# Output projection of a recurrent-memory attention in feature quarters, summed over all heads in PSUM, with a new instruction order

## The chip, the cores and the metric

The kernel runs on one core of one Trainium2 chip. The metric is device time in microseconds of one execution of the whole program, from the host's inputs in HBM to the output in HBM. A profiled execution gives, beside its own time, a span (first to last instruction) and a trace of every instruction and DMA packet. The engines are PE (TensorE, with its weight loads shown apart as PEld), DVE (VectorE), ACT (ScalarE), POOL (GpSimd) and SP (SyncE, which here only issues DMAs).

## The reference, cut to what matters

Two attentions read the same x (2048 tokens, 512 features) and a sigmoid gate mixes them. Attention A is recurrent: 64 segments of 32 tokens, one after the other, and eight memory rows that each segment hands to the next.

```python
for s in range(n_seg):                                # 64 segments of 32 tokens
    h = jnp.concatenate([mem, xs], axis=1)            # 8 memory rows + 32 tokens
    q = jnp.einsum('btd,dhe->bhte', h, Wq)            # 32 heads of 128; k and v likewise
    scores = jnp.where(mask, jnp.einsum('bhqe,bhke->bhqk', q, k) * scale, -1e9)
    o = jnp.einsum('bhqk,bhke->bhqe', _softmax(scores), v)
    o = jnp.einsum('bhte,hed->btd', o, Wo)            # the output projection
    mem = o[:, :M, :]                                 # to the next segment
    outs.append(o[:, M:, :])
# B: 32 heads of 16 in 4 blocks of 512 tokens, softmax plus a running linear memory, then @ wo
return g * a + (1 - g) * b                            # g = sigmoid((x * gate_w).sum(-1))
```

## The kernel before

**How A is tiled.** A segment's 40 rows are 8 memory rows and 32 tokens. Only 32 of them are in the recurrence for every step: 24 tokens and the 8 memory rows (tile `hT`, 512 features as 4 chunks of 128 by 32 columns). The last 8 tokens of a segment (the "rest") are projected for four segments at once (`p_rest`), outside the recurrence. Most matmuls use the array as four column groups of 32 (mode "c32"): the stationary operand has 32 columns, its product lands in PSUM partitions 32g to 32g+31, and four such matmuls run side by side. Mode "r32" splits the rows instead, mode "full" uses the array whole; an op with mode FLEX may take c32 (four times the instructions) or full.

**One segment (`p_seg`).** `project` computes k, q and v for two halves r of 16 heads each (`wproj`, line 1401: 16 matmuls of 512 columns per half). ACT or DVE copies each result to SBUF (`copy`, line 1001), DVE transposes 32x32 blocks (line 1466). `p_s` writes a mask product (`H`, from `hide` and `neg`) and adds the scores (`S`, lines 1481 and 1485); ACT takes exp into `PT`, 160 columns for the segment's own keys and 64 for the rest rows' keys. `p_u` sums over keys with a matmul against `ones` (`U`, line 1504), ACT forms the reciprocal as exp(-ln), DVE and POOL normalize `PT` (lines 1512, 1515). `PV` and `PW` (lines 1546, 1555) give the heads' outputs, copied to `OT`.

**The output projection (`wo`, line 1300).** Eight pieces, one for four heads each. For each head two matmuls of 256 columns go to column groups 2q and 2q+1, where q is the head's parity: even heads add up in PSUM partitions 0 to 63 (two feature halves of 32 rows), odd heads in 64 to 127. The two partial sums are then brought together in two ways. For the memory rows: a copy of the whole 128x256 result to SBUF (`par`), an f32 matmul against the small selection matrix `fold` that adds the halves and transposes (`fold`, line 1024 by way of `mm`, 16 weight loads and 16 matmuls in the trace), and a copy into the next `hT` (`hm`, line 1323). For the tokens: a DVE addition of both parts (`row`, line 1330) and a DMA to the DRAM tensor `a_rows`. The rest rows take the same `wo` with no fold.

**What orders the work.** The whole program is unrolled. Every op is declared once with what it reads and writes; the order of the ops on each engine is a compressed list, `ORDER`, that is decoded by `sequences`. Work of attention B (`bq`, `bk`, `bV`, `bL`, `bPV`, ...), of the rest rows (`rk`, `rq`, `rv`, `wor`) and of the output rows (`brow`) stands between the ops of the recurrence, so that PE has something to do while ACT and DVE work on the chain. A planner in `schedule` walks the given order with assumed costs, picks PSUM banks, and settles for a FLEX op whether it runs as c32 or full; among its constants are `LATENCY`, `TO_PE`, and, for PE's code, `BLOCK = 256`, `FETCH` and `FLOOD`: it assumes that PE passes a block of 256 instructions no faster than one in `FETCH` us (`FLOOD` while the weights are loaded).

```python
            at = (int((issued - self.BLOCK_AT) // self.BLOCK) + 1) * self.BLOCK + self.BLOCK_AT
            while at <= issued + n:
                tb = t + late + dur * (at - issued) / n
                if tb < last + wait:
                    late += last + wait - tb
```

Of the kernel before, what the change touches and what calls it, by code (L numbers as in the profile page):

```python
# [8 lines left out]
ALU = mybir.AluOpType  # L9
# [10 lines left out]
    "FP%vG5*AFh`)@=8NnCc#T7)p8{2I#Njbli?Ht<MlCV0E_2Lgd>Reicq#{zej<2(WYtcaYcfL=mzo<b^n`oQrt?4X=l0K|A;jYSjkffA_2MFVM6SfEMX^o@in&({YaCYOW$y`)p7D"  # L20
    "S`XiW8t_aqvKqjW{{7CHnNq!}ps?b<?`R*wI}B4o9BGDCQx}lccl|wAQsx#w{o02*@C?H*nhOpKFwQr|H)O2w?}{*(xL7i>^Ow;17;L=E6Uiuf7ORCqgCn5CVV*y)c>XNdyXQC&8"
    "+Y72_;!n^%v+zWkK>Q@Ko%!kq_yRP(Z#qJVwdIw8L)k~B$+4;xv_U_r96XPubB_I5D2!~a2}dp1JvLq@gWDhOdm=<**9v?sxJW25Ym?-ldeoxX!x`4-3l+>aiqjY*kKt=fdyyMrS"
    "TtKi`-Q|l8k2%X9cZ`c^&x5D1fH0$}`K-Y19{9|K0owjuuA~MQY~T9tV}(4D~NG=u6&MiY&(Y)ds*WfKih3Y5+XW8~DJ8n4rAi61zX|fPX3h>*sPY#?253SEIsV1Hk8!_{Fs%!nQ"
    "XbL@>yhz*P#id{eO=GyuC3I7pc!iC#F>x^|MNu9I~d942j2BKs}C{32?UUb0LFQ0ix-*wE`Wywhw40;SaxR(xH&0w&1~3r>%^+Q~*1w%X0dLK`~oRiUZ%v@YZ{<={$P$O>#Ht-g5"
    "W_?5ZV8Q)X6FKfa2uH#n*1->#gx`OOrGTS3=MBIgi05c@<lVI(bMKO(!P|IwkpyRX!0q9ky<A$_0F>qr~Z`i)*Pf7ko@^0+Ebu=O`6HS4D0zHsqF%|pCbq*x&7jftOc|B(>)Ul5$"
    "KZkl{cAySxd)nCa4`?xYI8Ydc-J`?j)*Ub>l_L53X(X=*iUSH*O)~7hZzt}07vPzsz=lT9d}LFYhY-VCz%g-Sk&Tdn#%}I-!r0;ryuSkmW=ndEhe6SCNkfQele4rTz@yN|bXC7X5"
    "{J?2%yvEGvj;w-nk4KLC-en4_WIY7iDIe*l{w;mHRx|tg>Hls*GGYd1hEQaKs1Q}WW<p1#~=%4@4Jyoy%+bJlSOafyRp_Xa4`#}?irSp1pk9MQq0GYpf9%!-z_SyD|7gBZ%B5TIq"
    "j09gbnawgKX$c#?|1Cs~gEHo!)LH84CffGH0VZT0$^?t^N$w830B|hK2#$tvh^^sW`y7ue)i_0Lx#2>;^cu>5W;-xd<!l97zIn;Kf(ek&7pZQ+7YB*SmTARuV{y-AwMMCKM1LYPP"
    "~))4IWaaGge4THwmP{^wvY!*lvJH(bT~67Xw$Rb#i-yJ6bZqrpAMCqpVq+CL^KX1>vZdW9hs0a&MX{9>MDOZ)R2yhq84)`!GpUJj{u>>cvyS0!<>j?=fe0?v}Q=Z<x@?wNUY$yZA"
    "zFPco@wd?LO2?m!oCp7uI?No{xf`T7mh(Vuka2P2NBjL6@&q4tn9-LUHbLvQ<mFTs0mU8w)fQ=)Tg95Y{pjmMvz9MhukU!<q>{^889C|HXya@J>msYn;Tl_Dv*39cH1&mo+Xe41Y"  # L30
    "-wSm-uVZSP0nU3c{&z|2*8u<9e)|_x{U6>^pl7v3#2Y5&Q0%_`roFvjdeSO!h*#aoFJaTRlWAg97R_;xOeeX3z-(9QdN}SDbR{UFCKc&eeOa*yIPK9s9P}2;t504CtmqX2Mw+iQ5"
    "@tKA=UflNik^qvi@F+4>L0)d(&!xk19$q(bRtIQWc@BSEx8e4y#yo$@6;zSCHbBOeZ<h6B!k<!-TSDxi4K*bikZ>pp~bl>Hqu#;4C5khfUzc#d<{t6?Px5m@jG!{EB_;XNdZ7Qa<"
    "_!tG*Vk&axoj=Q&KKgrGm_PfnATjB4lFLmlBPB8c|}{Fyc`a!-M(--zSkAhMb15|1nJS3ZI?~)7F2ydR(h4w*wifi(X$wk(c`}2lq(`n}~xm+tBe-phxR7hhP(F6%c_@3;2VOi8K"
    "0IWF}OGVoT9$D^z(mhuGUFN0eV{=&U*2KX%suN4|}cpN2o&L-b5#@Rdbk@U_Uld7ja8CV1^97EpLuk<t{Q59&T~*dNd`ZCe)KF;h&EwpriKdS!qG(~F?89a_L8NS*sgg4{@w?9l;"
    "feF-5D;?)*{K|f(}k-=ex`hV8A4~wYvlG_?UwX_CM;_f^|$mxlPvs==7yyp`s7Rb6~lv|=m<wQ*l<ksWBnG4WVTD%Uxy$`QF_L4ruWV>?|lmt;to=NS1Nc$BYcj!UB54s5&=+Z`h"
    "$6zq69SP2@b??e*C23Q(rlubAYG8Kh^MNI?GS<9D)_fw_W7&0PK8f;Cos*$W35lw;%+>UwMr<%PCrT1YJNla0KLRbALfVDbK>(VU0j1RCm9-9{rB@y*uHjiUFW9VgGA^-k;>dHxG"
    "eR$#lS^p{D*pQ~>17(+Y+@-b^rsDx*={Cnd=_*+90SJ#TY=UyiMCKojX!UJ6&GV|2aE<D0SLbUunkTR!|2Xm&PGX)kcZKF97ZT}|3r-1$3e-Nix|aRz^HYTOA*=4?*hl#4A`Q<ZC"
    ">FDSD|guH5?1h>+t@Kh*e)whO4?`H0f^525@Hd0T-*mLjqyP>Zv+DfZUo#u)sNO2r~5eQv&P&Ly2AwE(f_|I)F!!J~v>^Byd`RgNXacR6P4&@1ICR>mFv;8_2B&;xuq-jliAi1`y"
    "QiKxl(&bdbgm@+%jcTuWwH?C?}<KK;o+M`hp)fJ{ZBF7r)qa0}*7TT!AH2hLiAaNOmJ{L5hEUldHLZB8`Nn5fbf=aurgjSY9}=Cci-km(4F6>u<xnAt7S&d&da+`QD8Hd9m`@PAf"
    "i&U7Qf=7yxr3w`Wwpo`F{o4zP+#qf+-LpkzF1W7Mbg_W?J-#G-CU1lgEyDqw@ap8OrJFWol3c>aYFKUY7srBDZVKt_rXp-LnMRD2U5SJsTB_R9`RO)kp49l%cJ!fZ$&-=jhuD|L%"  # L40
    "y1IUvdzTEm-vL`Z29Oo8L4yauZ2~m^KkLz9E=C6p9~IB`Pd(L|p~L8+Bvv(^n2M(!qD_IvnXdOQgQ+LnC;oNI;()5(e;6J^Ix3=lKHKpkud&+*-qK+<?LAHz3IfD{nP3vL)m#`P%"
    "Az-nXxd79gj-ZTOY~ZssKMsNKbP{8mm>eCN5+d@bU9APlO@&%!)?+M1dv$KWu03m5O+^)TKirSE&UrOh#t1H282!iaJ?N_SyYf%rosL26SCQ=!v(yq47)#|vx&cv(H<$HgxXp=hZ"
    "2Rc&T>3VCqo>V5)bn`2h({Xl$<t=(LR4S4MVUe3V}q8op9@Lb$IR$pOxMuvL-je(~;MgBrrtSk<bU9BgVhTrgb}j!lAf@3|ZWb=ET&9xiA?8xV5(vQKl#k-ESru$T<VEo5RY5VB9"
    ";n)ICN-=;*U8u9Pxj8tCC-BpAUsZ37POobHh=y4yT`df2_XjG0)I&swks>^5Y!-}`l^h^wO7;Ovx5R<w~st3jh8jw7J5Y4EKg65tqoiZL5JL9r23)xZ{hUw@x3sEOV1pE~UFC`K~"
    "E6o~y85AcZW4>C!5R`4k0&Hh@U@drH+qp{ic1@XZ_Jev2;69t(qyI`J^5hYWAkuf?5K+7OejE>t4rV5PYOVAtN`!|>%h9}RpX5a|yrwrdb;8eW!--=b((!2GHnVQzU{=A<23o^Yq"
    "ca1cMH6dYhqqEO?+;p-pDh$~Ik?)QD4#mxwHD}i19fK}G^;8&n<-!kt*dcW=w`)kd<Q*$pWyEA{*?bvSf6i3q3T)N>8khzUn-Y=>b%GL;-a8w~x(uX6%4qkp4jh=4Ls<Ne^U*ga!"
    "{Gsyolt7waUkaOTHX1Wj80I!RG%`O#TeTRWz6O1O2x#+)X$7g(DRq0Y>ZZC1q){;eHD*WCUX`%YIE&>kHDlG;q2uoJb#J}aw0jc_Cm*<UxGR3UCxAYZZ+GIsZ4seqaiJjU+FFwa$"
# [90 lines left out]
class Slot(Res):  # L138
# [446 lines left out]
class Kernel:  # L585
# [837 lines left out]
    def p_seg(self, s):  # L1423
# [13 lines left out]
        def bank():  # L1437
            return P.slot("A")
# [178 lines left out]
```

## Time and profile before

| what | value |
|---|---|
| runs shown | 829.01, 830.72, 834.39 us; median 830.72 |
| profiled execution | 832.89 us, span 831.2 us, mean granted TensorE clock 0.998 |
| PE busy | 809.5 us (97%), 24474 matmuls |
| weight loads (PEld) busy | 521.5 us (63%), 24474 |
| DVE, ACT, POOL busy | 617.3, 562.9, 260.9 us (74, 68, 31%) |
| DMA queue q8 (PE's code) | 192 packets, 3.15 MB |
| first 60 us or so | the 16 MB of A's weights are loaded, 341 to 414 GB/s |

Busy time of PE is modelled: matmuls are pipelined, each is shown with its whole latency, and a stretch that reads as fully busy may still hold short stops. The weight loads (PEld) show those stops better, since each is short. "issue" as a releaser means that the engine waited for nothing that the profile shows.

### The profile page before, as it was taken

The numbers are of one execution on the slowest core, as the hardware profiler recorded it, in microseconds if no ns is written. First come the engines' busy times: TensorE is split into PE (matmuls) and PEld (weight loads), VectorE is DVE, ScalarE is ACT, GpSimd is POOL, SyncE is SP. The second block draws the span as 40 slices with busy tenths as digits, with TensorE's granted clock in tenths as the row PEclk, the third lists the DMA queues.
The fourth block names the chain that finished last, engine by engine and source line by source line (L and its number), as shares of the span: only waits on it lengthen the run. The fifth ranks groups of instructions, "written<-read, shape, count | busy, mean of one in ns | idle before, by whom it ended". The sixth has DMA issues, their size and how long they took to land.

```text
span 831.2 us, 53272 instructions
## 1 busy us (share of the span) xinstructions
PE 809.5 (97%) x24474; PEld 521.5 (63%) x24474; DVE 617.3 (74%) x1398; ACT 562.9 (68%) x1278; POOL 260.9 (31%) x576
## 2 busy tenths in 40 slices
PE   9999999999999999999999999999999999999987
PEld 4445666666666566666666666666766665666654
DVE  4688667768778768678676687776878767886776
ACT  3577676777766667776667766676656677767663
POOL 3443231323322332323233233423232223323340
PEclk9999999999999999999999999999999999999999
DMA  9983111121111111111011111100111100000001
GB/s 341 414 247 52 40 24 43 43 45 27 43 28 28 39 28 44 27 34 44 15 47 46 38 27 31 40 14 18 44 42 32 39 20 15 13 23 23 22 21 36
DMA packets 71701, 45.63 MB, mean 55 GB/s; under 512 B 50046, under 2 KB 69942, under 8 KB 69942
## 3 DMA queue, kind: packets, MB, share of 16 engines
q1 hardware_dynamic: 70422, 41.18, 17.5%
q8 instruction: 192, 3.15, 1.6%
q10 hardware_dynamic: 1056, 1.05, 0.4%
q14 instruction: 31, 0.25, 0.1%
HBM read 30.72 MB, written 8.87 MB: 48 GB/s over the span
## 4 chain that ended last, share of the span: by engine, by line
PE 87%; DVE 4%; ACT 3%; DMA 2%; issue 1%; SPq 1%; POOL 0%; DVEq 0%; POOLq 0%
PE pb L1401 47%; PE pb L1300 17%; PE pb L1024 7%; PE pb L1141 4%; PE pb L1026 2%; PE pb L1546 2%; PE pb L1182 2%; DMA st<-in_A_mem_dram 2%; PE pb L1504 2%; PE pb L1481 1%; PE pb L1230 1%; PE pb L1555 1%; DVE KT_sb L1466 1%; PE pb L1485 1%; ACT rc_sb L1510 1%
## 5 line engine op out<-in xcount | busy, mean ns | idle before, releaser
L1001 ACT ACTIVATE st<-pb 128x512 bf16<-128x512 f32 (+2 forms) x313 | 149.0, 494 | 103.0 <-PE pb L1401 78.0
L1159 ACT ACTIVATE PTB<-pb 128x640 bf16<-128x640 f32 x240 | 158.4, 703 | 37.2 <-PE pb L1141 32.5
L1401 PE MATMUL pb<-Wv_sb,hT 128*32 128x512 bf16 x2048 | 162.8, 381 | 0.2 <-DVE ao L1330 0.2
L1401 PE MATMUL pb<-Wq_sb,hT 128*32 128x256 bf16 (+1 forms) x3072 | 138.0, 308 | 0.1
L1300 PE MATMUL pb<-Wo_sb,OT_sb 128*32 128x256 bf16 x4096 | 132.8, 273 | 3.0 <-issue 1.9
L1401 PE MATMUL pb<-Wk_sb,hT 128*32 128x512 bf16 x2048 | 132.0, 379 | 0.1
L1300 PEld LDWEIGHTS pb<-Wo_sb,OT_sb 128*32 128x32 bf16 x4096 | 100.7, 96 | 18.4 <-ACT OT_sb L1001 4.3
L1165 POOL TENSOR_SCALAR_AFFINE_SELECT PTB<-PTB 128x512 bf16<-128x512 bf16 x120 | 77.6, 647 | 107.4 <-ACT PTB L1159 100.8
L1515 POOL TENSOR_TENSOR PT_sb<-PT_sb,rc_sb 128x64 bf16<-128x64 bf16 x90 | 33.1, 367 | 248.9 <-ACT rc_sb L1510 240.5
L1401 PEld LDWEIGHTS pb<-Wq_sb,hT 128*32 128x32 bf16 x3072 | 82.5, 97 | 39.1 <-issue 0.8
L1466 DVE STREAM_TRANSPOSE QT_sb<-st 128x256 bf16<-128x256 bf16 (+1 forms) x192 | 94.4, 510 | 16.7 <-ACT st L1001 15.1
L1466 DVE STREAM_TRANSPOSE KT_sb<-st 128x512 bf16<-128x512 bf16 x128 | 89.4, 700 | 11.6 <-ACT st L1001 9.5
L1001 ACT ACTIVATE OT_sb<-pb 128x320 bf16<-128x320 f32 (+1 forms) x140 | 58.1, 428 | 37.9 <-PE pb L1555 36.3
L1401 PEld LDWEIGHTS pb<-Wk_sb,hT 128*32 128x32 bf16 x2048 | 57.0, 97 | 42.4 <-ACT PTB L1159 1.1
L1001 DVE CAST OT_sb<-pb 128x320 bf16<-128x320 f32 (+1 forms) x120 | 56.8, 478 | 31.3 <-PE pb L1555 29.3
L1401 PEld LDWEIGHTS pb<-Wv_sb,hT 128*32 128x32 bf16 x2048 | 52.2, 98 | 18.8 <-DVE ao L1330 0.7
L1508 ACT ACTIVATE rc_sb<-pb 128x160 f32<-128x160 f32 x128 | 38.8, 303 | 36.3 <-PE pb L1504 35.3
L1323 DVE CAST hT<-pb 128x32 bf16<-128x32 f32 x63 | 12.0, 191 | 66.4 <-PE pb L1024 66.1
L1489 ACT ACTIVATE PT_sb<-pb 128x224 bf16<-128x224 f32 x128 | 45.6, 356 | 17.4 <-PE pb L1485 12.8
L1001 DVE CAST V_sb<-pb 128x512 bf16<-128x512 f32 x65 | 44.5, 685 | 9.9 <-PE pb L1401 9.0
L1512 DVE TENSOR_TENSOR PT_sb<-PT_sb,rc_sb 128x160 bf16<-128x160 bf16 x128 | 42.7, 334 | 8.2 <-ACT rc_sb L1510 6.7
L1001 ACT ACTIVATE stg<-pb 128x512 bf16<-128x512 f32 (+1 forms) x68 | 37.9, 559 | 14.3 <-PE pb L1401 10.2
(203 smaller groups left out, 1472.3 us busy)
## 6 DMA issues: line engine op xcount, KB each, us to landing
Wv_sb<-in_A_Wv_dram SPq DMA_DIRECT2D x4, 1024.0 KB, 11.8
Wk_sb<-in_A_Wk_dram SPq DMA_DIRECT2D x4, 1024.0 KB, 21.0
Wq_sb<-in_A_Wq_dram SPq DMA_DIRECT2D x4, 1024.0 KB, 26.9
Wo_sb<-in_A_Wo_dram SPq DMA_DIRECT2D x4, 1024.0 KB, 20.9
rest_v<-stg SPq DMA_DIRECT2D x112, 32.0 KB
rem_v<-rest_v SPq DMA_DIRECT2D x28, 128.0 KB, 2.6
a_rows<-ao SPq DMA_DIRECT2D x63, 32.0 KB
stg<-a_rows SPq DMA_DIRECT2D x15, 128.0 KB
```

Source lines behind the costliest of these rows:

```text
L1001: self.P.op(("act", "dve"), (lambda a: a.activation(dst, src(), ACT.Copy), lambda d: d.tensor_copy(dst, src())), reads=reads, writes=write ...
L1024: ins = pe.matmul(out[32 * c:32 * c + 32], lhsT[:, 32 * c:32 * c + 32], rhs, start=start, stop=stop, tile_position=(0, 32 * c), **kw)
L1141: ins = pe.matmul(pb[slot.banks[i]][:, base + a - lo:base + b - lo], KT[r0:r1, 128 * kc:128 * kc + 128], Q[r0:r1, t0 + a:t0 + b], start=Tr ...
L1159: P.op("act", (lambda dst=dst, src=src: lambda a: a.activation(dst, src(), ACT.Exp, scale=0.25))(), reads=[pair], writes=["%s%d_%d" % (nam ...
L1165: P.op("gp", (lambda pt=pt, ii=ii: (lambda g: g.affine_select(pt, pt, ([[0, len(ii)]] if len(ii) > 1 else []) + [[1, 128]], ALU.is_ge, 0.0 ...
L1300: ins = pe.matmul(pb[so.b][p0:p0 + 32, 0:256], tok(r, g, l), self.Wo[:, h, 256 * d:256 * d + 256], start=(r == 0 and g == 0 and l < 2), st ...
L1401: ins = pe.matmul(self.pb[sl.b][32 * g:32 * g + 32, 0:hi - lo], x[:, c, 0:32], cols, start=(c == 0), stop=(c == C - 1), tile_position=(0, ...
L1466: op("dve", (lambda dst=dst, src=src: lambda d: d.transpose(dst, src))(), reads=["st%d%s" % (i, tag)], writes=["%sT%d%s" % (kind, r, tag)] ...
L1489: op("act", lambda a: a.activation(PT[:, r, :], pb[rb.b][:, 0:224], ACT.Exp, scale=SCALE), reads=[rb], writes=["PT%d" % r, "PT%dr" % r], n ...
L1508: op("act", lambda a: a.activation(rc[:, r, :], pb[rb.b][:, 0:160], ACT.Ln), reads=[rb], writes=[rr], name="ln%d_%d" % (s, r), cost=t_act( ...
L1512: op("dve", lambda d: d.tensor_tensor(PT[:, r, 0:160], PT[:, r, 0:160], rc[:, r, :], ALU.mult), reads=[rp, rr], writes=[rp], name="nrm%d_% ...
L1515: op(("dve", "gp"), tuple((lambda e: e.tensor_tensor(rest, rest, late(rc[:, r, :]), ALU.mult)) for _ in range(2)), reads=[rp + "r", rr], w ...
```

## The change

- **Output projection of the segments 0 to 62:** for each head four matmuls of 128 columns, one into each column group. Group d holds feature quarter d, and all 32 heads add up in the same PSUM partitions. Quarters are interleaved blocks of 32 features: `Wo` is read as `(m d i) -> d, m, i`. `par`, `fold` and the addition `row` go away. In their place DVE transposes the 128x128 result in 32x32 blocks out of PSUM (`turn`), DVE or POOL copies 8 columns of each block into the next `hT` (`hm`), and ACT or DVE copies the result to `ao` (`row`), which is stored with the quarters apart; `p_tail` puts the features back in order as it scales. The rest rows and the last segment keep two matmuls of 256 columns for each head.
- **Scores:** `PT` and its PSUM bank are laid out by head, 56 columns each (16 for the rest rows, 40 for the segment's own), and the mask product `H` covers 160 columns, not 224.
- **Gate:** the gate's matmuls run in c32 with x moving, 128 columns each, and a DVE transpose (`gate_t`) follows.
- **Start:** `dma_x` is given the first place in the queue, B's first weights are loaded for 384 of 512 columns, the loads of `mem0` and of single weight chunks change places.
- **Order and planner:** a new `ORDER` for all engines, and new constants, with `FETCH` from 3.6 to 2.5.

```diff
 ORDER = (
...
-    LATENCY = {"pe": 0.22, "act": 0.04, "dve": 0.04, "gp": 0.1, "sp": 2.0}
+    LATENCY = {"pe": 0.23, "act": 0.05, "dve": 0.05, "gp": 0.1, "sp": 2.0}
...
-    FETCH = 3.6
-    FLOOD = (52.0, 6.3)
+    FETCH = 2.5
+    FLOOD = (52.0, 4.6)
...
-        self.hide = t("hide_sb", [128, 224])
+        self.hide = t("hide_sb", [128, 160])
...
-            dma(self.g_wB[k], (lambda k: lambda s: s.dma_start(self.wB[k], self.B_w[k].rearrange("(c p) n -> p c n", p=128)))(k),
+            dma(self.g_wB[k], (lambda k: lambda s: s.dma_start(self.wB[k][:, :, 0:384], self.B_w[k].rearrange("(c p) n -> p c n", p=128)[:, :, 0:384]))(k),
...
-                  writes=[rs], name="dma_x%d_%d" % (sb, i), prio=prio - 1.5, load=0.4, cost=0.45 if sb or i else 1.2)
+                  writes=[rs], name="dma_x%d_%d" % (sb, i), prio=-110 + 0.1 * i, load=0.35 if i else 2.9, cost=0.45)
...
+            for c in range(C):
+                part = xT[:, c, :].rearrange("p (i b t) -> p b i t", i=4, b=4)
+                for b in range(4):
+                    ins = pe.matmul(pb[sg.b][32 * b:32 * b + 32, 0:128], self.gw[:, c, :], part[:, b], start=(c == 0), stop=(c == C - 1),
+                                    tile_position=(0, 32 * b))
...
+        def part_of(h, n, d):
+            w = self.Wo[:, h, :]
+            return w[:, 256 * d:256 * d + 256] if late is None else w.rearrange("p (m d i) -> p d m i", d=4, i=32)[:, 4 // n * d:4 // n * d + 4 // n]
...
-                        for d in range(2):
-                            p0 = 64 * q + 32 * d
-                            ins = pe.matmul(pb[so.b][p0:p0 + 32, 0:256], tok(r, g, l), self.Wo[:, h, 256 * d:256 * d + 256], start=(r == 0 and g == 0 and l < 2),
+                        for d in range(4 if mem else 2):
+                            p0 = 32 * d if mem else 64 * q + 32 * d
+                            ins = pe.matmul(pb[so.b][p0:p0 + 32, 0:128 if mem else 256], tok(r, g, l), part_of(h, 4 if mem else 2, d),
...
-        self.copy(part, lambda: pb[so.b][:, 0:256], 256, [so], rhl, "par%s" % name, prio)
-        if mem:
-            def f_fold(pe, m):
...
-                    ins = self.mm(pe, m, pb[so.b][:, 256 + 16 * c:272 + 16 * c], part[:, 128 * c:128 * c + 128], self.fold[:, :], True, True)
...
-        P.op("dve", lambda d: d.tensor_tensor(ao[:, :], pb[so.b][0:64, 0:256], part[64:128, :], ALU.add), reads=[so] + rhl, writes=[rao],
-             name="row%s" % name, cost=0.45, prio=late)
+        if mem:
+            turned = self.rc[:, 0, 0:128]
+            P.op("dve", lambda d: d.transpose(turned, pb[so.b][:, 0:128]), reads=[so], writes=["rc0"], name="turn%s" % name, cost=0.31, prio=prio)
+            P.op(("dve", "gp"), tuple((lambda v: v.tensor_copy(mem[0], turned.rearrange("p (c t) -> p c t", t=32)[:, :, 24:32])) for _ in range(2)),
+                 reads=["rc0"], writes=[mem[1]], name="hm%s" % name, cost=(0.14, 0.27), prio=prio)
+            self.copy(ao[:, 0:128], lambda: pb[so.b][:, 0:128], 128, [so], [rao], "row%s" % name, late)
+            return self.g_ao[b], ao[:, 0:128], rao
...
-                        ins = pe.matmul(pb[rb.b][32 * g:32 * g + 32, l * L:(l + 1) * L], KT[:, 16 * r + 4 * g + l, :], QT[:, 16 * r + 4 * g + l, :],
+                        ins = pe.matmul(pb[rb.b][32 * g:32 * g + 32, 56 * l + 16:56 * l + 56], KT[:, 16 * r + 4 * g + l, :], QT[:, 16 * r + 4 * g + l, :],
...
-            op("dve", lambda d: d.tensor_tensor(PT[:, r, 0:160], PT[:, r, 0:160], rc[:, r, :], ALU.mult), reads=[rp, rr],
+            op("dve", lambda d: d.tensor_tensor(mine[r], mine[r], by_head(rc[:, r, :]), ALU.mult), reads=[rp, rr],
```

More of the change, by code (lines that the diff above doesn't have):

```diff
@@ L20 @@
[L20 to L23, printed above, removed]
@@ L670, in alloc @@
         self.rdram0 = nc.dram_tensor("rest_v0", [64, H * self.E], BF16)
[L671 to L672 removed]
+        self.ao = [t("ao%d" % i, [128, 256]) for i in range(2)]
         self.OTr = t("OTr_sb", [128, H, 32])
```

218 lines of the change are left out of this document (109 added, 109 removed).

## The prediction

> **What bounds the kernel now.** I read the page first: the share of each engine, the chain that ended last, and the DMA queues.
>
> ```profile
> span 831.2 us, 53272 instructions
> PE 809.5 (97%) x24474; PEld 521.5 (63%) x24474; DVE 617.3 (74%) x1398; ACT 562.9 (68%) x1278; POOL 260.9 (31%) x576
> PE 87%; DVE 4%; ACT 3%; DMA 2%; issue 1%; SPq 1%; POOL 0%; DVEq 0%; POOLq 0%
> q8 instruction: 192, 3.15, 1.6%
> ```
>
> PE is the bound: 97% busy and 87% of the chain. So a chain of waits that gets shorter is worth little by itself; what counts is time that PE no longer spends, and anything that stops PE. The last row is the one that this change turns on. Queue q8 brings PE's code: 192 packets for 24474 weight loads and 24474 matmuls, 48948 instructions, so 255 instructions a packet (256, with the waits), 16.4 KB each. Its share, 1.6% of 16 engines over 831.2 us, is 213 us, 1.1 us a packet on its engine.
>
> Next the time line of the weight loads, for PE's stops that no semaphore explains, and the busy time by windows between those stops (columns: window, its length, then busy time and count for PE and PEld first).
>
> ```profile
> 446.51 0.45 PEld L1024 LDWEIGHTS pb<-V,phiK 128*32 128x32 bf16 x15
> 447.49 0.09 PEld L1024 LDWEIGHTS pb<-V,phiK 128*32 128x32 bf16 x1 [0.53 <-issue]
> 451.26 0.09 PEld L1401 LDWEIGHTS pb<-Wq_sb,xr 128*32 128x32 bf16 x1 [0.20 <-issue]
> 455.17 0.11 PEld L1024 LDWEIGHTS pb<-xT,wqB_sb 128*32 128x32 bf16 x6 [0.22 <-issue]
> 564.47 0.45 PEld L1300 LDWEIGHTS pb<-Wo_sb,OT_sb 128*32 128x32 bf16 x20 [1.14 <-issue]
> ```
>
> ```profile
> 266.35:269.85 3.50, 3.50 (x143) 2.15 (x134) 3.25 (x8) 2.18 (x7) 1.32 (x3) 1.00 0.02 5
> 447.49:451.26 3.77, 3.74 (x125) 2.80 (x124) 3.15 (x10) 2.77 (x9) 0.68 (x2) 1.00 0.04 9
> 451.26:455.17 3.91, 3.91 (x131) 2.60 (x129) 2.60 (x6) 3.18 (x8) 1.90 (x4) 1.00 0.22 38
> 559.69:564.47 4.78, 3.92 (x128) 2.30 (x127) 2.26 (x7) 3.41 (x7) 0.99 (x3) 1.00 0.26 58
> ```
>
> ```profile
> q8 instruction: 1, 0.02, 1.9%
> ```
>
> The stops come in the middle of one op: 15 of 16 loads, then nothing for half a microsecond, then the sixteenth. No data can be missing there. Between one stop and the next lie 124 to 129 load and matmul pairs, one packet of code, and the window from 447.6 to 451.3 holds exactly one code packet (the last row, of the DMA view). So PE has run out of code: it passes one packet's worth, and the next is not there sooner than about 3.8 to 3.9 us after the last crossing (4.8 in the worst row). The row at 266.35 shows a packet's worth that went by in 3.50 us with no stop at its end. I take **3.5 us** as the time that one packet needs; 3.2 and 3.9 are the ends I carry. Now the segments:
>
> ```profile
> 88.56:799.00 710.44, 698.93 (x21960) 460.83 (x21962) 534.85 (x1202) 497.56 (x1137) 220.11 (x475) 1.00 0.13 32
> 467.99:471.89 3.90, 3.90 (x93) 2.57 (x88) 1.75 (x4) 3.03 (x7) 0.64 (x1) 1.00 0.34 76
> 471.89:475.39 3.50, 3.50 (x125) 2.05 (x118) 2.25 (x6) 2.72 (x9) 0.50 (x2) 1.00 0.03 5
> 475.39:480.18 4.79, 4.79 (x169) 3.80 (x165) 4.48 (x12) 2.97 (x7) 1.17 (x4) 1.00 0.13 31
> ```
>
> ```profile
> L1323 DVE CAST hT<-pb 128x32 bf16<-128x32 f32 x59 | 11.3, 191 | 61.5 <-PE pb L1024 61.2
> ```
>
> The first and last row cover 59 segments: 12.0 us and 372 pairs each, 744 instructions, 2.9 packets, one every 4.1 us. The three middle rows split one segment at its first projection, its first mask product H, its first PV and the next projection. In the first stretch 256 instructions last 5.4 us (128/93 x 3.90), in the second 3.6, in the third, with PV and the output projection, 3.6. Code is just in time now, and in the dense stretches it has no slack.
>
> **The change part by part.** *The fold.* It leaves with its 16 loads and 16 matmuls for each of 63 segments.
>
> ```profile
> 466.34 0.38 ACT L1001 ACTIVATE st<-pb 128x256 f32<-128x256 f32 x1 [0.19 <-PE pb L1300]
> 466.90 0.22 PEld L1024 LDWEIGHTS pb<-fold_sb,st 128*32 128x32 f32 x16
> 467.29 0.19 DVE L1323 CAST hT<-pb 128x32 bf16<-128x32 f32 x1 [0.82 <-PE pb L1024]
> 467.99 1.49 PE L1401 MATMUL pb<-Wq_sb,hT 128*32 128x512 bf16 x32
> ...
> L1024 PEld LDWEIGHTS pb<-fold_sb,st 128*32 128x32 f32 x1008 | 16.0, 110 | 13.4 <-ACT st L1001 8.7 <-DVE st L1001 1.9 <-issue 0.4
> L1330 DVE TENSOR_TENSOR ao<-pb,st 64x256 bf16<-64x256 f32 x63 | 26.2, 416 | 1.9
> L1218 DVE STREAM_TRANSPOSE t_sb<-pb 128x512 f32<-128x512 f32 x32 | 22.6, 706 | 2.5 <-PE pb L1182 2.5
> ```
>
> PE is rid of 16.0 us of loads at least, and of 16.0 + 13.4 = 29 if all the idle time before them goes too. Most of that idle time is a change of array mode that the next op pays in its place; I take 16 + 4 = **20 us**. The chain copy, fold, copy (466.34 to 467.5) becomes a transpose and a copy. A 128x128 transpose out of PSUM is not in the trace; four times its width takes 0.71 us (L1218), so 0.18 to 0.4, and the chain gets some 0.6 us shorter. That is not added: PE has projections of B and the rest between the last `wo` and the first projection, and these have to be done anyway. The addition (0.42 us on DVE) goes, a narrower copy takes its place; DVE, at 74%, gets no fuller, and an op queued behind `turn` waits no longer than it did behind the addition.
>
> *The projection itself.* Sixty-four matmuls of 256 columns become 128 of 128. The same columns stream, so the question is what a short one costs.
>
> ```profile
> 477.03 1.93 PE L1300 MATMUL pb<-Wo_sb,OT_sb 128*32 128x256 bf16 x64
> L1300 PE MATMUL pb<-Wo_sb,OT_sb 128*32 128x256 bf16 x4096 | 132.8, 273 | 3.0 <-issue 1.9 <-DVE OT_sb L1001 0.8 <-ACT OT_sb L1001 0.2
> 662.12 0.40 PE L1024 MATMUL pb<-wvB_sb,xT 128*32 128x128 bf16 x16
> L1024 PE MATMUL pb<-wvB_sb,xT 128*32 128x128 bf16 x368 | 8.6, 219 | 0.0
> ```
>
> Now (1.93 - 0.273) / 63 = 26 ns each; B's v projection has the new shape, (0.40 - 0.219) / 15 = 12 ns each. So 1.7 us before and 1.5 to 1.7 after. I take **0**, with 6 us either way (0.1 us for each of 63).
>
> *Smaller edits.*
>
> ```profile
> L1024 PE MATMUL pb<-hide_sb,neg_sb 128*32 128x224 bf16 x504 | 34.8, 259 | 0.0
> L934 PEld LDWEIGHTS pb<-gw_sb,xT 128*128 128x128 bf16 x64 | 2.0, 96 | 0.8 <-issue 0.6
> L1512 DVE TENSOR_TENSOR PT_sb<-PT_sb,rc_sb 128x160 bf16<-128x160 bf16 x128 | 42.7, 334 | 8.2 <-ACT rc_sb L1510 6.7
> 0.79 1.83 SPq L917 DMA_DIRECT2D PTB<-in_A_x_dram  x4
> GB/s 341 414 247 52 40 24 43 43 45 27 43 28 28 39 28 44 27 34 44 15 47 46 38 27 31 40 14 18 44 42 32 39 20 15 13 23 23 22 21 36
> ```
>
> H loses 64 of its 224 columns: at 26 ns for 256 columns 504 x 6.5 ns = **3 us**. The gate can save no more than its 2.8 us; **1**. The normalization and `PW` now walk `PT` in strides; a stride could cost up to 0.1 us at each of 126 places on the chain, but V's and B's matmuls stand beside it: 0, at worst 8 us. "x first" finds x first already: its loads are issued at 0.79 us, ahead of all others on SP. The three shorter loads of B's weights spare 0.39 MB, 1 us of transfer at the 341 to 414 GB/s of the first 40 us; between 0 and 1, I take 0.
>
> These sum to 20 + 3 + 1 = **24 us less for PE**, between 10 and 36. If code came in time, the profiled 832.9 us would be 809.
>
> *The code.* The projection adds 64 pairs for each of 63 segments, the fold takes 16 away: 48 pairs, 96 instructions more, 840 for each segment, 3.3 packets, on the whole 24474 + 63 x 48 = 27498 pairs, 215 packets. At 12.0 - 0.4 us for a segment that is one every 3.5 us on the average, all that the wall allows, and the dense part is far over it. All 96 land in the third stretch: 2 x 169 + 96 = 434 instructions in some 4.5 us (4.79 less the fold), 256 in 2.65 us. I read the new order list out against the ops: between PV and the next projection stand 445 instructions on the average of the segments, 355 before, so the new order does not spread them. With the second stretch (250 in 3.45 us) that makes 684 instructions in 7.95 us, 2.97 us for a packet's worth. Of the 2.67 packets there, one on the average straddles the thin first stretch and has slack; 1.67 lie wholly inside and are each short by 3.5 - 2.97 = 0.53 us. That is 0.9 us a segment, **55 us** over 62 segments. With 3.2 us for a packet it is 0.38 us a segment, 24 us; with 3.9 it is 1.55, 96 us. Nothing hides this: a stop in code holds all of PE, and PE is the bound. What goes late next is everything behind it on PE, and through `hT` the next segment.
>
> The Trainium skill speaks against this term: Runtime: NRT & Kernel Launch, section Instruction fetch mechanics, has the sequencer fetch the next 16 KiB block of 256 instructions while it runs the present one, and calls the cost of crossing a block boundary "mostly hidden". The 16.4 KB and 255 instructions agree with the trace; "hidden" does not agree with the stops at 447.49, 451.26 and 455.17 us. By that sentence the term would be 0 and the sum 809 us.
>
> **The sum** against the profiled execution: 832.9 - 24 + 55 = 864 us. That execution lies 2.2 us above the median of the runs (830.72), so **862 us** for the timed runs.
>
> **The rivals.**
> 1. *Code keeps up* (faster). Stops at code boundaries are rare so far, and none of the rows shows how short a packet's turn can be when PE always wants it; the planner now reckons with 2.5 us, under the 2.65 of the third stretch. Then only the savings count: 809, against a median 807 to 812. Against it: three stops in a row at 3.8 to 3.9 us. It decides at 2.65 us for a packet.
> 2. *A packet takes 3.2 us on the average* and loss and gain cancel: 832.9 - 24 + 24 = 833, no change. For it: the 3.50 us row ended in no stop. Against it: every stop seen was longer.
> 3. *The starved pace is the rule.* Once PE has run dry, each following packet takes 3.9 us, as at 455.17: 832.9 - 24 + 96 = 905.
>
> **How the numbers follow.** The forecast has 0.68; it covers 3.3 to 3.75 us for a packet, 842 to 888 us. Rival 3 has 0.13, rival 2 0.07, rival 1 0.12. The range takes in rival 2 and reaches to just under rival 3: 832 to 902 us. A measurement of this kernel can tell about 1% from no change (the three runs lie 0.65% apart): faster by more 0.12 (rival 1), within 1% 0.07 (rival 2), slower 0.81.
>
> **What would show it.** Right: some 215 q8 packets; stops "<-issue" of 0.2 to 1 us in the weight loads, most in line 1300's new form or the ops just after it, one or two for each segment and 50 us in all; packets' worths of 128 pairs that last 3.4 to 3.9 us right after one another; no fold; some 27500 matmuls, the 128-column form at 12 to 14 ns. Wrong: packets' worths that pass in 2.5 to 3 us with no stop, and a segment of 11.6 us.

## The result and the profile after

The changed kernel takes 904.15 us (median of four runs, 901.6 to 910.2) against 831.16 us for the kernel before on the same chip: a ratio of 1.0885, 95% interval 1.082 to 1.095. It is 73 us slower. The forecast was 862 us with a range to 902; the time fell just outside, beside rival 3 (905).

From the page of the changed kernel: span, engines, the chain that ended last, and the queue that brings PE's code.

```profile
span 899.9 us, 59653 instructions
PE 813.5 (90%) x27669; PEld 539.7 (60%) x27669; DVE 625.6 (70%) x1453; ACT 541.2 (60%) x1235; POOL 255.5 (28%) x566
PE 85%; issue 9%; DVE 4%; ACT 1%; POOL 0%; DVEq 0%; POOLq 0%
q8 instruction: 217, 3.56, 1.7%
```

PE works as long as before (813.5 us against 809.5), but its share of the span fell from 97 to 90%, and the chain holds 9% of "issue" where it held 1%. Little else grew: ACT is less busy than before, DVE is busy for 8 us more. The code is 217 packets, 25 more.

The view of waits names the place (columns: engine, tile and line, releaser; total us, count, longest).

```profile
PEld pb L1308 <- issue: 64.9, 59, 2.4
PEld pb L1407 <- issue: 20.6, 40, 1.8
PEld pb L1143 <- issue: 14.3, 43, 0.4
```

Line 1308 is the output projection, line 1300 before; line 1143 is a product of attention B, line 1141 before. The same view of the kernel before (line 1546 is PV):

```profile
PEld pb L1300 <- issue: 2.8, 3, 1.3
PEld pb L1141 <- issue: 7.1, 24, 0.7
PEld pb L1546 <- issue: 4.9, 18, 0.4
```

Not every wait for "issue" is a stop for code: nearly all of B's (line 1143) and those of PV in the kernel before are short and do not stand at the ends of packets. The time line of the output projection's weight loads shows the form of the stops, and the windows from one crossing to the next show what lies between them.

```profile
477.22 0.45 PEld L1308 LDWEIGHTS pb<-Wo_sb,OT_sb 128*32 128x32 bf16 x31 [0.49 <-issue]
481.27 0.72 PEld L1308 LDWEIGHTS pb<-Wo_sb,OT_sb 128*32 128x32 bf16 x49 [1.98 <-issue]
494.09 0.18 PEld L1308 LDWEIGHTS pb<-Wo_sb,OT_sb 128*32 128x32 bf16 x12 [0.72 <-issue]
497.75 0.33 PEld L1308 LDWEIGHTS pb<-Wo_sb,OT_sb 128*32 128x32 bf16 x21 [1.25 <-issue]
```

```profile
473.42:477.22 3.80, 3.33 (x129) 2.31 (x129) 2.56 (x7) 3.15 (x10) 0.78 (x2) 1.00 0.22 47
477.22:481.27 4.05, 2.25 (x127) 1.74 (x126) 0.81 (x2) 1.98 (x5) 1.46 (x4) 1.00 0.51 133
490.22:494.09 3.87, 3.32 (x128) 2.42 (x127) 2.92 (x9) 2.71 (x7) 1.03 (x3) 1.00 0.03 6
494.09:497.75 3.66, 2.59 (x127) 1.91 (x127) 1.55 (x5) 2.23 (x4) 0.59 (x2) 1.00 0.02 4
```

Each window holds one packet's worth, 126 to 129 pairs, and lasts 3.66 to 4.05 us. In the second one PE had work for 2.25 us of the 4.05 and stood for 1.8 (the weight loads, which end earlier, for 1.98).

To size this, I counted the gaps of over 0.15 us that stand ahead of every 256th instruction in PE's order. Counted with the semaphore instructions that the trace shows in PE's stream (299 in the changed kernel), they stand at place 193 or 194 of 256 from the first packets to the last. In the kernel before they add up to 8.8 us, in the changed one to **98.0 us** in 107 stops, some 60 us of them inside line 1308's `Wo_sb,OT_sb`. What is left of the span is 822.4 us before and 801.9 after. So the change does two things: it saves 20.5 us of work and adds 89 us of waiting for code.

The groups of the new operations, split by form:

```profile
L1308 PE MATMUL pb<-Wo_sb,OT_sb 128*32 128x128 bf16 x8064 | 151.0, 220 | 52.1 <-issue 51.3 <-DVE PT_sb L1523 0.5
L1329 DVE STREAM_TRANSPOSE rc_sb<-pb 128x128 f32<-128x128 f32 x63 | 20.0, 317 | 101.7 <-PE pb L1308 101.7
L1026 PE MATMUL pb<-hide_sb,neg_sb 128*32 128x160 bf16 x504 | 34.1, 233 | 0.1
L1523 DVE TENSOR_TENSOR PT_sb<-PT_sb,rc_sb 128x160 bf16<-128x160 bf16 x128 | 44.1, 344 | 10.3 <-ACT rc_sb L1521 8.4
```

The `turn` takes 317 ns and waits for PE alone. The strided normalization takes 344 ns where it took 334.

### The profile page after: what moved, and what is told of

Its sections match the earlier page's. It is cut to its first block, busy times and chain, and to the rows that moved or that the text cites. A ratio compares the mean times of both kernels' runs of the same rounds, so it can differ in the third digit from the quotient of the medians.

```text
span 899.9 us, 59653 instructions
## 1 busy us (share of the span) xinstructions
PE 813.5 (90%) x27669; PEld 539.7 (60%) x27669; DVE 625.6 (70%) x1453; ACT 541.2 (60%) x1235; POOL 255.5 (28%) x566
## 3 DMA queue, kind: packets, MB, share of 16 engines
q8 instruction: 217, 3.56, 1.7%
## 4 chain that ended last, share of the span: by engine, by line
PE 85%; issue 9%; DVE 4%; ACT 1%; POOL 0%; DVEq 0%; POOLq 0%
PE pb L1407 45%; PE pb L1308 18%; PE pb L1026 6%; PE pb L1143 3%; PE pb L1556 2%; PE pb L1184 2%; PE pb L1028 2%; PE pb L1492 2%; PE pb L1515 1%; PE pb L1565 1%; PE pb L791 1%; PE pb L1496 1%; PE pb L1232 1%; ACT V_sb L1003 0%; ACT rc_sb L1521 0%
## 5 line engine op out<-in xcount | busy, mean ns | idle before, releaser
L1308 PE MATMUL pb<-Wo_sb,OT_sb 128*32 128x128 bf16 (+1 forms) x8128 | 153.0, 220 | 52.1 <-issue 51.3
L1003 ACT ACTIVATE st<-pb 128x512 bf16<-128x512 f32 (+1 forms) x250 | 124.6, 518 | 116.0 <-PE pb L1407 113.2
L1308 PEld LDWEIGHTS pb<-Wo_sb,OT_sb 128*32 128x32 bf16 x8128 | 125.8, 97 | 76.6 <-issue 58.2
L1407 PE MATMUL pb<-Wq_sb,hT 128*32 128x512 bf16 (+1 forms) x3072 | 144.7, 308 | 4.2 <-issue 2.3
L1407 PE MATMUL pb<-Wk_sb,hT 128*32 128x512 bf16 x2048 | 136.0, 379 | 0.4 <-issue 0.2
L1407 PEld LDWEIGHTS pb<-Wq_sb,hT 128*32 128x32 bf16 x3072 | 86.8, 97 | 46.8 <-issue 7.8
L1003 ACT ACTIVATE OT_sb<-pb 128x320 bf16<-128x320 f32 (+2 forms) x143 | 59.3, 428 | 55.6 <-PE pb L1565 54.3
L1329 DVE STREAM_TRANSPOSE rc_sb<-pb 128x128 f32<-128x128 f32 x63 | 20.0, 317 | 101.7 <-PE pb L1308 101.7
L1407 PEld LDWEIGHTS pb<-Wk_sb,hT 128*32 128x32 bf16 x2048 | 62.0, 97 | 38.8 <-issue 3.0
L1454 POOL COPY QT_sb<-rem_q 128x256 bf16<-128x256 bf16 x64 | 28.5, 445 | 80.5 <-PE pb L1496 66.2
L1003 DVE CAST V_sb<-pb 128x512 bf16<-128x512 f32 x66 | 44.7, 677 | 4.3 <-PE pb L1407 3.7
## 6 DMA issues: line engine op xcount, KB each, us to landing
Wv_sb<-in_A_Wv_dram SPq DMA_DIRECT2D x4, 1024.0 KB, 10.6
Wo_sb<-in_A_Wo_dram SPq DMA_DIRECT2D x4, 1024.0 KB, 20.5
```

The source lines that it names most:

```text
L1003: self.P.op(("act", "dve"), (lambda a: a.activation(dst, src(), ACT.Copy), lambda d: d.tensor_copy(dst, src())), reads=reads, writes=write ...
L1308: ins = pe.matmul(pb[so.b][p0:p0 + 32, 0:128 if mem else 256], tok(r, g, l), part_of(h, 4 if mem else 2, d), start=(r == 0 and g == 0 and ...
L1407: ins = pe.matmul(self.pb[sl.b][32 * g:32 * g + 32, 0:hi - lo], x[:, c, 0:32], cols, start=(c == 0), stop=(c == C - 1), tile_position=(0, ...
L1454: op("gp", lambda g: g.tensor_copy(QT[:, :, SEG:L], Qr), reads=[rQr], writes=["qTr"], name="qr%d" % s, cost=0.47, prio=s - 0.3)
```

## Experiments

**1. The same projection with half the instructions.** The changed kernel, its segments' projection put back into 64 matmuls of 256 columns.

```diff
-                        for d in range(4 if mem else 2):
-                            p0 = 32 * d if mem else 64 * q + 32 * d
-                            ins = pe.matmul(pb[so.b][p0:p0 + 32, 0:128 if mem else 256], tok(r, g, l), part_of(h, 4 if mem else 2, d),
+                        for d in range(2):
+                            p0 = 64 * q + 32 * d
+                            ins = pe.matmul(pb[so.b][p0:p0 + 32, 0:256], tok(r, g, l), part_of(h, 2, d),
...
```

> The changed kernel, with only its output projection in the 63 segments put back into 64 matmuls of 256 columns (even and odd heads apart) in place of 128 of 128 columns: the same columns streamed, 128 instructions fewer in each segment. The sums of even and odd heads are not added, and half of the columns are not read, so the output lacks them; everything else (no fold, one transposition, the gate, H, the layout of P, the loads, the order) is the changed kernel's. Theory C (the loss is the time in which PE waits for its code): 851-128 = 723 instructions a segment need 2.8 packets, 11.1 us at the spacing of 3.92 us seen between stopped crossings, under the 12.5 us that a segment takes without stops, so the time falls from 904 to some 813 us (808 to 825), under the kernel before. Theory O (the loss is the new order, the transposition in the chain, or one of the other edits): 895 to 910 us, as the changed kernel.

```profile
span 828.5 us, 51589 instructions
q8 instruction: 185, 3.03, 1.5%
PEld pb L1308 <- issue: 9.2, 19, 1.5
```

Measured: 826.72 us, a ratio to the kernel before of 0.9961 (0.9938 to 0.9983). The new order, the transpose, `H`, the gate and the loads are all still there, and the 73 us lost are gone, with 4 more: the loss hangs on the splitting of the projection, which changes the number of PE's instructions and not the columns, and not on any other edit. My number was some 14 us too low, since the stops did not all go: 21.7 us are left.

**2. The same split in the kernel before.** Each 256-column matmul of the segments' projection becomes two of 128; fold, additions and the old order stay.

```diff
+                            for c0, n in ((0, 128), (128, 128)) if mem else ((0, 256),):
-                            ins = pe.matmul(pb[so.b][p0:p0 + 32, 0:256], tok(r, g, l), self.Wo[:, h, 256 * d:256 * d + 256], ...
+                                ins = pe.matmul(pb[so.b][p0:p0 + 32, c0:c0 + n], tok(r, g, l), self.Wo[:, h, 256 * d + c0:256 * d + c0 + n], ...
```

> The kernel before, with only each of the 64 matmuls of 256 columns of a segment's output projection split into two of 128 columns (63 segments): the same columns, the same sums, the fold and the old order kept; 128 instructions more in each segment. Theory C (code): 750+128 = 878 instructions need 3.43 packets, 13.4 us at 3.92 us each, over the 12.85 us that a segment of the kernel before takes without stops; with stops that sit unevenly as in the changed kernel the time rises by 60 to 100 us, to 890 to 930 us. Theory O (short matmuls are as good as long ones, and the loss comes from the other edits): 829 to 838 us.

```profile
span 920.1 us, 61336 instructions
q8 instruction: 224, 3.67, 1.7%
PEld pb L1301 <- issue: 53.3, 44, 2.2
PEld pb L1024 <- issue: 14.3, 12, 1.9
L1301 PE MATMUL pb<-Wo_sb,OT_sb 128*32 128x128 bf16 x8064 | 143.9, 220 | 46.2 <-issue 43.8 <-ACT PTB L1159 0.9 <-DVE OT_sb L1001 0.8
```

Measured: 919.42 us, ratio 1.1082 (1.1034 to 1.113). (Unlike what the expectation says, this kernel does not keep all of its sums, so its output is not the reference's; the work of PE is the one meant.) The split alone, in the old order and with nothing else of the change, costs 89 us. Of these 94.4 - 8.8 = 86 are stops at packets' ends, most in line 1301, 8.5 us in the fold behind it (line 1024, which also serves other products). What is left of the span without stops, 825.7 us against 822.4, says that the short matmuls themselves cost 3 us.

**3. Half the dose.** The changed kernel with the four-quarter form in even segments alone.

```diff
+        four = mem and int(name) % 2 == 0
...
-                        for d in range(4 if mem else 2):
+                        for d in range(4 if four else 2):
...
```

> The changed kernel with the 128-column projection in the even segments and the 64 matmuls of 256 columns in the odd ones (whose output lacks the sums, as in the run with all segments so). 787 instructions a segment on average. Theory C1 (code is short locally: a stop belongs to the dense stretch in which it falls, whatever came before): half of the loss, so 904 - 0.5 x 91 = 858 us (848 to 870). Theory C2 (code is short on average: what counts is the supply over two segments, 787 x 3.92/256 = 12.05 us against 12.5): most of the loss goes, 815 to 838 us. Theory O: 895 to 910 us.

```profile
span 868.8 us, 55685 instructions
PEld pb L1309 <- issue: 39.5, 44, 2.3
```

Measured: 866.21 us, ratio 1.0416 (1.039 to 1.0442). This is C1's number: half the segments, half the loss (39.5 of the 77.4 us between run 1 and the changed kernel). Segments with few instructions do not pay for their neighbours; the supply doesn't reach from one segment into the next. Stops: 64.9 us, the rest of the span 803.9.

**4. As many instructions more in another place.** In the kernel before, the 512-column matmuls of `k` and `v` become two of 256. The planner, which counts instructions with `Count`, does not see the split.

```diff
+                        two = name[0] in "kv" and hi - lo == 512 and not isinstance(pe, Count)
+                        for lo2, hi2 in ((0, 256), (256, 512)) if two else ((0, hi - lo),):
+                            ins = pe.matmul(self.pb[sl.b][32 * g:32 * g + 32, lo2:hi2], x[:, c, 0:32], part2, ...
```

> The kernel before with 128 instructions more in each segment, as many as the run that splits the output projection, but in another place: the matmuls of 512 columns of the segments' k and v projections are split into two of 256 (same columns, same sums, old order). Theory C1 (what counts is the supply in the stretch itself): 128 pairs of 256 columns stream in 3.5 us (27 ns each), and the stretch by PE alone with 256 columns needed 3.75 us for 256 instructions, so such a stretch is short by only some 0.25 us a packet: about 2 packets a segment in these stretches, 0.3 to 0.6 us, 20 to 40 us in all at most; 835 to 865 us. Theory C2 (what counts is the number of instructions over the whole segment): as the split of the output projection, 919 us. Theory O (the number of instructions costs nothing): 829 to 836 us.

```profile
span 906.2 us, 61446 instructions
PEld pb L1404 <- issue: 33.3, 60, 1.9
PEld pb L1300 <- issue: 18.8, 32, 1.4
PEld pb L1549 <- issue: 12.3, 41, 0.9
```

Measured: 907.57 us, ratio 1.094 (1.0918 to 1.0963). C1's 20 to 40 us missed by twice and more, and C2 (919) is not far. The rows show what C1 left out: the projection at line 1300, whose instructions are those of before, stops for 18.8 us where it stopped for 2.8, and PV at line 1549 for 12.3 (line 1546 before, 4.9 us); 5.2 us of PV's are now at packets' ends, where it had none before. Of the 33.3 us of line 1404, which holds all projections, some 16 are in the split matmuls themselves. So most of the new stops fall in ops that the edit did not touch. I read this so: the long matmuls of `k` and `v` were where the packet for the dense part came in early; made dense, they stop themselves and hand the next stretch no lead. Inside a segment the lead then does carry over, while from segment to segment it doesn't (run 3). How far it carries was not measured.

**5. The price of a packet by itself.** PE alone, 1024 pairs for each width.

```python
for n in WIDTHS:                     # 128, 192, 256, 288, 320, 384, 512; then once more beside 48 loads of 1 MB
    for i in range(1024):
        p = 32 * (i % 4)
        pe.matmul(ps[p:p + 32, 0:n], w[:, p:p + 32], x[:, 0:n], start=True, stop=True, tile_position=(0, p))
```

> Not the reference's computation (the output is zeros): PE alone runs 14 stretches of 1024 pairs of weight load and matmul of 32 output rows, turning through the four column groups, of 128, 192, 256, 288, 320, 384 and 512 columns, first with no other transfer, then the same seven with 48 loads of 1 MB beside. 256 instructions are 128 pairs. By the row of 128 columns of the changed kernel (12 to 14 ns a pair by itself) 128 pairs stream in 1.7 us, of 256 columns in 3.5, of 512 in 7. Theory C at the measured spacing: in the quiet stretches every packet takes 3.8 to 3.9 us for 128, 192 and 256 columns, and its streaming time from 288 columns on; theory C at the price that I had predicted: 3.5 us. Beside the loads more, 4 to 5 us, if the traffic of other transfers is what spreads the spacing between 3.4 and 5.9 us in the changed kernel. A crossing that is hidden: 1.7 us for 128 columns.

The windows of its stretches (window, length, busy time and count of PE and PEld; at the end the clock, the DMA share and GB/s): the six narrower widths without loads, in order (the first window holds the start of the program), then 128 and 192 columns beside the loads. Below them the time line of the weight loads, without and with loads.

```profile
0.32:32.80 32.48, 17.54 (x1019) 16.63 (x1023) 3.91 (x3) 0.11 (x4) 1.00 0.02 4
32.80:61.96 29.16, 22.54 (x1040) 21.13 (x1032) 0.00 (x0) 0.00 (x0) 1.00 0.02 4
61.96:91.94 29.98, 28.96 (x1034) 27.77 (x1029) 0.00 (x0) 0.00 (x0) 1.00 0.02 4
91.94:123.28 31.34, 31.34 (x1036) 31.34 (x1028) 0.00 (x0) 0.00 (x0) 1.00 0.02 5
123.28:158.02 34.74, 34.74 (x1034) 34.74 (x1026) 0.00 (x0) 0.00 (x0) 1.00 0.02 4
158.02:199.57 41.55, 41.55 (x1035) 41.55 (x1027) 0.00 (x0) 0.00 (x0) 1.00 0.01 3
254.72:300.06 45.34, 23.26 (x1030) 21.97 (x1025) 0.00 (x0) 0.00 (x0) 0.77 0.98 398
300.06:350.09 50.03, 28.76 (x1038) 27.16 (x1030) 0.00 (x0) 0.00 (x0) 0.84 1.01 418
```

```profile
14.62 1.82 PEld L36 LDWEIGHTS ps<-x_sb,w_sb 128*32 128x32 bf16 x128 [1.88 <-issue]
18.35 1.82 PEld L36 LDWEIGHTS ps<-x_sb,w_sb 128*32 128x32 bf16 x128 [1.90 <-issue]
22.08 1.83 PEld L36 LDWEIGHTS ps<-x_sb,w_sb 128*32 128x32 bf16 x128 [1.90 <-issue]
...
275.15 1.82 PEld L36 LDWEIGHTS ps<-x_sb,w_sb 128*32 128x32 bf16 x128 [2.94 <-issue]
281.35 3.41 PEld L36 LDWEIGHTS ps<-x_sb,w_sb 128*32 128x32 bf16 x128 [4.38 <-issue]
```

With 128 columns the 128 pairs of a packet are through in 1.82 us, and then PE stands for 1.9: in the rows shown, one packet every 3.73 us. Single packets take either 3.45 or 3.73 us, and the five between 14.62 and 32.44 us take 3.56 on the mean. With 192 and 256 columns the eight packets take 29.2 and 30.0 us, 3.65 and 3.75 each (the 256 columns alone need 3.5, and single packets there take up to 4.0), so the width hardly matters. From 288 columns on nothing stops, and the time is that of the columns (3.92, 4.34, 5.19 us a packet). That is a wall of about **3.6 to 3.75 us**, a little over the 3.5 that I took. Expected were 3.8 to 3.9; those are too long, and "hidden" is out for narrow matmuls. Beside loads at 400 GB/s it is 5.7 and 6.3 us, where I expected 4 to 5. The granted clock was lower in these two windows (0.77 and 0.84), but PE's own pace does not make this time: in the slowest row the 128 loads are through in 3.41 us, and PE then stands on.

By the times of the crossings and of the code packets in the DMA records, a packet's 3.7 us without loads are three waits in a row: 1.1 us from the crossing to the start of the next packet's transfer, 1.15 us of transfer, 1.4 us until PE goes on. Beside the loads they are 3.7, 1.05 and 1.4: the transfer is no longer than before, only its start is late.

**6. Which traffic lifts the price.** As run 5 with 128 columns, and a load after every 64 pairs: 0, 32, 64, 128, 256, 512 and 1024 KB.

> Not the reference's computation (the output is zeros): PE alone in seven stretches of 1024 pairs of 128 columns, 8 packets each, with one load from DRAM started after every 64 pairs: of 0, 32, 64, 128, 256, 512 and 1024 KB. In the first such run a packet took 3.65 to 4.07 us with nothing beside and 5.65 to 6.27 beside loads at 420 GB/s. Theory T (the traffic of the kernel is what lifts 3.7 to 3.9): about 3.7 us at 0 KB, 3.8 to 4.0 at 64 and 128 KB (the kernel's mean is 51 GB/s), rising to 5 to 6 at 1024 KB. Theory Q (only a full queue matters): 3.7 us up to 256 KB, then a jump. If small loads cost nothing, the changed kernel's 3.92 us between stops must come from its own gaps, not from the supply.

```profile
33.93:65.08 31.15, 18.02 (x1039) 16.75 (x1030) 0.00 (x0) 0.00 (x0) 0.89 0.10 21
65.08:94.09 29.01, 15.77 (x1040) 14.60 (x1032) 0.00 (x0) 0.00 (x0) 1.00 0.15 41
94.09:122.82 28.73, 15.77 (x1040) 14.60 (x1032) 0.00 (x0) 0.00 (x0) 1.00 0.27 77
122.82:152.92 30.10, 15.76 (x1040) 14.60 (x1032) 0.00 (x0) 0.00 (x0) 1.00 0.44 141
152.92:184.94 32.02, 18.34 (x1040) 17.05 (x1032) 0.00 (x0) 0.00 (x0) 0.89 0.80 253
184.94:240.62 55.68, 23.42 (x1045) 21.75 (x1033) 0.00 (x0) 0.00 (x0) 0.70 0.91 350
```

Theory Q (the stretch without loads holds the start and is not shown; 8 packets a window): with 21, 41, 77 and 141 GB/s beside it a packet takes 3.89, 3.63, 3.59 and 3.76 us, with no trend; 253 GB/s make it 4.0, and only the full queue jumps (in the last window the eight packets take 44.7 us, 5.6 each; the rest is the final store). In the stretch without loads the five packets between 14.07 and 33.53 us take 3.89 on the mean, where run 5, in an execution on another chip, had 3.56 for the same width. So the spread from one stretch to the next is as large as anything that loads up to 141 GB/s do, and the kernel's 51 GB/s don't lift the price.

What lengthens the mean of 3.91 us (median 3.79) between a crossing and a stop at the next in the changed kernel shows in its DMA records. Of 90 such stops of over 0.3 us, 56 have a code packet whose transfer starts at most 1.3 us after the crossing, much as in run 5, and there the next crossing comes after 3.68 us on the mean. For 24 the transfer starts over 1.5 us after, and the next crossing comes after 4.5 us. Other traffic just ahead of the start is about the same for both (11 and 13% of the DMA engines' time); PE had waited somewhat longer for other engines behind the crossing, 0.2 us against 0.1. So the supply by itself is that of runs 5 and 6, and a late start of the transfer makes the long ones. What makes the start late is not shown.

**7. One small edit alone.** The kernel before with the 160-column mask and the tiles by head.

> The kernel before with one part of the change alone: the mask H written over 160 columns instead of 224, and the score and probability tiles laid out by head (the strided P). Prediction's step: H gives 3 us, the strides cost 0 to 8; so 828 us, between 826 and 836. If the strides cost what the changed kernel's rows show (344 ns against 334 for the normalisation on DVE, 378 against 367 on POOL), nothing of that is seen in the end.

Measured: 828.50 us, ratio 0.9987 (0.9973 to 1.0002). The direction is as expected, and the span without stops fell from 822.4 to 820.7 us: a gain of 1.5 us or so, not to be told from none, and no loss by the strides.

**8. A version meant to beat both.** As run 7, with the fold in bf16 in place of f32.

```diff
-        self.fold = t("fold_sb", [128, 16], F32)
+        self.fold = t("fold_sb", [128, 16])
-        part = hl[:, :].bitcast(F32)
+        part = hl[:, 0:256] if mem else hl[:, :].bitcast(F32)
```

> A version meant to beat both: the kernel before with the narrow H as in the run of that part alone, and with the fold kept but its input copied as bf16 and its matrix in bf16, so that its matmuls need one pass instead of several and fewer instructions (48.3 thousand on PE instead of 49.3). Theory C: the fold's price falls by some 6 us, H gives 3, the stops at code boundaries (9 us before) stay or fall: 820 us, between 814 and 826. If the chain through the copy and not PE's time sets the fold's price: 827 us.

Measured: 829.84 us, ratio 1.0012 (0.9995 to 1.0029): nothing gained. The span without stops is 817.9 us, 4.5 less than before, as the first half of the expectation has it; but the stops went from 8.8 to 13.0 us, though there are 16 instructions fewer in each segment. It looks as if PE now reaches its crossings earlier and the code does not. No version that I ran and that keeps all sums is faster than the kernel before; run 1's 0.4% is that of a kernel that leaves sums out.

**All of it by one number.** I took from each trace the times of the crossings without their stops and replayed them with a single rule: no crossing sooner than p after the one before it (from 55 us on, behind the first loads). The spans are those of the pages, the rest is worked out from the traces.

| kernel | code packets | span | stops | span less stops | replay, p = 3.5 | 3.75 | 3.9 |
|---|---|---|---|---|---|---|---|
| before | 192 | 831.2 | 8.8 | 822.4 | 0 | 4.9 | 12.5 |
| changed | 217 | 899.9 | 98.0 | 801.9 | 65 | 94 | 114 |
| 1, 256 columns again | 185 | 828.5 | 21.7 | 806.8 | 10 | 22 | 32 |
| 2, split in before | 224 | 920.1 | 94.4 | 825.7 | 78 | 106 | 126 |
| 3, half the segments | 201 | 868.8 | 64.9 | 803.9 | 43 | 64 | 79 |
| 4, `k` and `v` split | 224 | 906.2 | 78.1 | 828.1 | 45 | 76 | 99 |
| 7, mask alone | 192 | 828.9 | 8.2 | 820.7 | 0 | 5.4 | 13 |
| 8, bf16 fold | 188 | 830.9 | 13.0 | 817.9 | 4.4 | 12.9 | 21 |

The column without stops falls into two families, 818 to 828 with the fold and 802 to 807 without it; all else between these kernels is stops. And 3.75 us, a price within what the stretches of runs 5 and 6 took (3.56 to 3.89), gives the stops of seven kernels within 4 us and of one (run 2) within 12. Within that spread it was chosen: with 3.6, what run 5 had where PE was short of code throughout, the changed kernel's replay gives some 75 us of the 98. The replay uses each kernel's own trace, so it shows that one wall is enough, not that it must be, and the wall is not sharp: two packets' worths of the changed kernel passed in 2.97 (at 194.64) and 2.61 us (at 659.06) with no stop, and there the next transfer had started 0.6 and 0.2 us after the crossing, not 1.1. That the stops come with the instructions is shown by runs 1, 2 and 4.

## Why the prediction was wrong, step by step

- **The mechanism** was right: PE out of code, stops "<-issue", most of them in line 1300's new form. Runs 1 and 2 show it from both sides. Forecast were 215 packets and 27498 matmuls; there are 217 and 27669.
- **The step that failed is the code term,** 55 us, where 98.0 - 8.8 = 89 us of new stops were measured. Two things in it were too small.
- **The first is the price of a packet,** 3.5 us. I took it from one row that passed in 3.50 us without a stop, though every stopped crossing that the prediction shows stood at 3.77 or more. It is the shortest row of its trace. In run 5 single packets take 3.45, 3.73 or 4.0 us, so one row that is not stopped is one draw at best; its transfer had also started 0.9 us after the crossing, where run 5 has 1.05 to 1.16. By my own formula 3.75 gives (3.75 - 2.97) x 1.67 = 1.30 us a segment, 81 us over 62 segments instead of 55. By itself that would still have lain inside the forecast's spread, whose upper end, 888 us, stands for 3.75.
- **The second** is the way to sum it. I let an average segment be short by an average. Segments differ, and a packet in hand early gives back nothing from one segment to the next (run 3): the replay with my own 3.5 gives 65 us where the formula gave 55, and with 3.75 94 where it gives 81.
- **The savings** came out as 20.5 us for 24 forecast. `H` gave some 1.5 for 3, not to be told from none, and no cost of the strides was seen (run 7). The 128-column form lies inside its 6 us either way: run 2 has it at +3.3, the changed kernel against run 1 at -4.9. The fold's 20 us was not run by itself; with these it is left as the main part. One reading behind it was wrong: I put most of the 13.4 us of idle time before the fold's loads down to a change of array mode, but the row shown there has 10.6 of them ended by the copy to `st` (ACT 8.7, DVE 1.9). The gate, the loads and the place of x were not tried one by one.
- **The new sum:** 832.9 - 20.5 + 89 = 901.4 us, and the profiled execution took 901.6. Both terms come from that execution, so this closes the account and tests nothing.
- **Stops** were to be one or two a segment, 0.2 to 1 us each; there are 107 in 64 segments, 0.9 us on the mean and 2.4 at the longest.
- **Rival 3** had the time (905) by luck. It has 3.9 us for a packet once PE has run dry. That number is the measured mean of 3.91 between stops, but run 5 has no second, slower pace: PE ran dry at each crossing and stayed at 3.45 to 3.73. Its code term of 96 us was 7 too large and the savings that it shared with the forecast 3.5 too large, so half of the one error is taken back by the other.
- **Rival 1,** code hidden, fails for narrow matmuls. The Trainium skill, Runtime: NRT & Kernel Launch, section Instruction fetch mechanics, speaks of only two 16 KiB lines of code (and, in another sentence, of 128 KiB for PE) and of fetches hidden behind the issue of instructions. The trace agrees with the two lines: in run 5's starved stretches the next transfer starts 1.1 us after a crossing, and no further packet is in hand. It agrees with "hidden" only where 256 instructions last longer than the packet's 3.6 to 3.75 us; at 128 columns PE issues them in 1.82.

## What to carry to other kernels

Count PE's instructions as a resource: 256 of them, 128 pairs of load and matmul, cost 3.6 to 3.75 us on the mean in run 5, 28 or 29 ns a pair. In four column groups, matmuls of 256 columns or fewer therefore stopped for code there and those of 288 did not, and a split that streams the same columns is not free. Look at the stops that no semaphore explains, at every 256th instruction, before adding any; by run 4, a stretch of long matmuls ahead of a dense one seems to be what feeds it, so it isn't free room either. And take the price of a resource from a run in which it alone is short, not from the shortest row of a trace in which it is mostly not.

## What was not expected of the hardware

- A code packet's 3.45 to 3.73 us in run 5 hold only 1.15 us of transfer on the mean; the other 2.5 us are waiting ahead of it and behind it, and they come anew for each packet.
- Other transfers don't slow the code until the DMA engines are nearly full: 3.6 to 3.9 us up to 141 GB/s (0.44 busy), 4.0 at 253 (0.80), 5.6 at 350 (0.91). In run 5, beside loads at 400 GB/s, the start of the fetch is late (3.7 us for 1.1), not its transfer.
